# Attention and channel mix in one kernel: new load order, new engine orders, casts moved to GpSimd

## The chip, the cores and the metric

The kernel runs on one core of a Trainium2 chip. Its time is the device time of one launch in microseconds (us). The engines are TensorE (PE; PEld is its weight load), VectorE (DVE), ScalarE (ACT), GpSimd (POOL) and SyncE (SP, which issues the DMAs here). Each engine runs its own instructions strictly in the order in which the program lists them, and waits on semaphores for what other engines and DMAs produce.

## The reference

Windowed attention with a few sink positions is followed by a gated channel mix with a token shift. There are 4 batches, 8 heads, 768 positions, head size 64; the window is 128, and the first 4 positions are seen by all.

```python
scores = scale * np.matmul(q, k.transpose(0, 1, 3, 2))
keep = is_sink | in_window
a = softmax(np.where(keep, scores, -1e9))
x = np.matmul(a, v)                     # to (B, S, H * D)
x_prev = shift(x)                       # one position back, zero first
xk = mu_k * x + (1.0 - mu_k) * x_prev
xr = mu_r * x + (1.0 - mu_r) * x_prev
k = np.maximum(xk @ w_k, 0.0)
v = k * k @ w_v
out = 1.0 / (1.0 + np.exp(-(xr @ w_r))) * v
```

Inputs and output are float32; the kernel computes in bfloat16 with float32 accumulation.

## The kernel before, in words

The work is cut into 12 units of 256 positions, three to each batch. A unit goes through these steps, with the lines of the kernel before:

- load: q, k and v of the unit come by DMA from SP's queue, two DMAs of 256 KB each (v at L304; k and q at L334, or at L314 where a DMA transposes them later: k from unit 4 on, q from unit 8 on). The weights w_k, w_r, w_v come in five DMAs of 1 MB (L351).
- prepare: casts to bfloat16 of k and q (L540, L533: tiles kb and qb) and of v (L643: vb). k and q are transposed on PE with a copy out of PSUM (L573, L586: kt and qt), or by DMA (L559).
- attend: scores on PE into a pair of PSUM tiles (L718), the exponential on ACT (L772, tile e), the mask on DVE (L786), values on PE (L805) with a column of ones that gives the sum, its reciprocal and the product on DVE (L819, L822, tile x). The sink positions add scores (L693, L700) and values (L760), and come from a spread of v (L673, L677).
- mix: x is transposed on PE (L846) and copied to xt (L855), or by DMA for the last three units (L866). DVE makes the difference td of neighbours (L874) and xk and xr from it (L885).
- ffn: the keys product (L936), a relu (L946 on ACT, L950 on DVE), its square (L964 on ACT, L960 on DVE, tile kk), the gate product (L976) with a tanh (L982), the values product (L994; L906 for the very last half), the gating on DVE (L1003; L916) and the store (L1010; L921).

The weights are cast to bfloat16 at L498 (ACT), L502 and L504 (DVE, POOL).

All these steps are recorded as numbered operations (Plan.op) in the order of the program text, and issued in another order, which the table ORDER lists by number; a planner wrote it down ahead of time, and nothing of the planner is left in the kernel. CHOICE names the engine for operations that have several (alts), by number. SLOTS gives the buffer of each taken tile. Since every engine and queue works in order, only the order within each engine matters in ORDER. A negative number in ORDER stands for a matmul of zeros into one of four PSUM banks (Plan.fill, L1014), which computes nothing that is used. PSUM holds two pairs of banks for scores (pool sc) and four single banks (pool bank).

Operations 0 to 3 are the loads of k and q of unit 0; 4 and 5 are v of unit 0; 6 to 9 are k and q of unit 1; 10 and 11 are the two loads of w_k.

Of the kernel before, what the change touches and what calls it, by code (L numbers as in the profile page):

```python
# [18 lines left out]
    90: "ACT", 91: "ACT", 92: "ACT", 93: "ACT", 95: "ACT", 97: "ACT", 99: "ACT", 100: "DVE",  # L19
    103: "DVE", 108: "DVE", 109: "POOL", 111: "DVE", 112: "ACT", 113: "ACT", 139: "DVE", 142:  # L20
    "DVE", 144: "DVE", 145: "DVE", 148: "DVE", 151: "DVE", 154: "DVE", 196: "POOL", 199: "POOL",
    202: "POOL", 206: "DVE", 223: "DVE", 227: "DVE", 228: "ACT", 278: "DVE", 283: "DVE", 284:
    "POOL", 287: "ACT", 288: "DVE", 300: "DVE", 309: "ACT", 313: "ACT", 320: "DVE", 356: "DVE",
    358: "POOL", 363: "POOL", 366: "ACT", 367: "ACT", 369: "DVE", 389: "ACT", 446: "DVE", 447:
    "ACT", 527: "DVE", 548: "ACT", 552: "ACT", 555: "DVE", 560: "ACT", 595: "DVE", 597: "DVE",
    600: "POOL", 602: "DVE", 605: "ACT", 606: "DVE", 628: "ACT", 636: "ACT", 677: "POOL", 681:
    "DVE", 683: "DVE", 684: "DVE", 702: "ACT", 706: "ACT", 710: "ACT", 714: "ACT", 753: "DVE",
    759: "DVE", 761: "ACT", 782: "DVE", 783: "ACT", 787: "ACT", 791: "ACT", 795: "ACT", 832:
    "DVE", 838: "ACT", 839: "ACT", 859: "ACT", 866: "DVE", 867: "ACT", 906: "POOL", 912: "DVE",
    914: "ACT", 915: "DVE", 931: "ACT", 935: "ACT", 939: "ACT", 943: "ACT", 1000: "DVE", 1004:  # L30
    "DVE", 1005: "ACT", 1008: "DVE", 1009: "ACT", 1028: "DVE", 1037: "ACT",
# [116 lines left out]
class Plan:  # L148
# [23 lines left out]
    def run(self):  # L172
        keys = [(name, key) for o in self.ops for name, key in o["take"]]
        for (name, key), slot in zip(keys, SLOTS, strict=True):
            self.buf[key] = self.pools[name][slot]
# [8 lines left out]
def kernel(  # L184
# [14 lines left out]
    nc = tc.nc  # L199
# [14 lines left out]
    P = Plan()  # L214
# [854 lines left out]
```

## Time and profile before

| what | value |
|---|---|
| three runs | 167.81, 171.39, 171.4 us, median 171.39 |
| the profiled execution, from its first instruction to its last | 167.6 us (the profile gives no other time of it) |
| granted TensorE clock | 0.999 |
| DMA packets | 79042, 34.60 MB |

The table of busy times and the views of the profile stand in the prediction. In the views by stage each engine has its busy time and, in brackets, its count of instructions. In the list of groups a row holds line, engine, operation, tiles, shape and count, then busy time and mean duration in ns, then idle time just before the group's instructions and what ended it. In the chain of waits and in the timeline the first two numbers are start and duration in us; x2 means that two instructions that follow each other are merged. In a row of one tile, three durations with slashes are least, median and most, in ns.

### The profile page before, as it was taken

What the parts mean: (1) busy time and instruction counts of PE and PEld (TensorE: products, weight loads), DVE (VectorE), ACT (ScalarE), POOL (GpSimd) and SP (SyncE); (2) the same over time, 40 slices, a digit from 0 to 9 for tenths busy, and PEclk for the clock granted to TensorE, in tenths of its full rate; (3) what the DMA queues carried; (4) which work ended last, traced back from release to release, by engine and by line L of the source; (5) the groups of instructions that cost most, each with busy time, mean ns of one, the idle gap of its engine ahead of it and who ended that gap; (6) DMA issues with size and microseconds to landing.
All of it is one profiled execution on the core that took longest, in us unless ns stands there. A gap on an engine that the chain in (4) does not pass through costs nothing.

```text
span 167.6 us, 4210 instructions
## 1 busy us (share of the span) xinstructions
PE 159.7 (95%) x1601; PEld 102.4 (61%) x1601; DVE 146.2 (87%) x375; ACT 133.4 (80%) x221; POOL 16.6 (10%) x43
## 2 busy tenths in 40 slices
PE   6999997999999999899999999999999999999991
PEld 1447574755558576676556885665765576764850
DVE  5189999999999999899999999989798799998821
ACT  4269998999999997999879999989799829614340
POOL 6423021005000010022000000010010000000000
PEclk9999999999999999999999999999999999999999
DMA  4999989999899999979999999999997774131303
GB/s 102 300 327 369 346 172 312 372 324 328 189 248 166 204 294 224 253 153 133 218 256 149 214 239 174 233 219 200 211 189 185 194 162 155 63 66 63 125 0 125
DMA packets 79042, 34.60 MB, mean 206 GB/s; under 512 B 67112, under 2 KB 73520, under 8 KB 79024
## 3 DMA queue, kind: packets, MB, share of 16 engines
q1 hardware_dynamic: 79008, 34.35, 92.0%
q8 instruction: 12, 0.20, 0.5%
q14 instruction: 6, 0.05, 0.1%
q10 hardware_dynamic: 16, 0.00, 0.0%
HBM read 24.12 MB, written 6.29 MB: 181 GB/s over the span
## 4 chain that ended last, share of the span: by engine, by line
PE 58%; DVE 11%; DMA 11%; SPq 7%; ACT 7%; issue 3%; ACTq 0%; DVEq 0%
PE bank L936 18%; PE bank L994 18%; PE bank L976 8%; DMA vs<-in_v_dram 6%; SPq L334 5%; PE sc L718 4%; PE bank L805 4%; DMA qs<-in_q_dram 3%; ACT e L772 3%; DMA qt<-qb 2%; DVE ob L1003 2%; DVE e L786 2%; PE bank L846 2%; DVE x L822 2%; PE bank L573 2%
## 5 line engine op out<-in xcount | busy, mean ns | idle before, releaser
L936 PE MATMUL bank<-xk,wk_sb 128*128 128x256 bf16 x384 | 48.1, 273 | 0.1
L994 PE MATMUL bank<-wv_h,kk 128*128 128x512 bf16 x184 | 46.4, 379 | 0.0
L772 ACT ACTIVATE e<-sc 128x1024 bf16<-128x1024 f32 (+1 forms) x48 | 45.4, 974 | 1.2 <-PE sc L718 1.2
L936 PEld LDWEIGHTS <-wk_sb 128*128 128x128 bf16 x384 | 36.2, 98 | 7.6 <-issue 0.7
L786 DVE TENSOR_TENSOR e<-e,mask 128x1024 bf16<-128x1024 bf16 (+1 forms) x48 | 30.7, 655 | 0.7 <-ACT e L772 0.5
L946 ACT ACTIVATE rl<-bank 128x512 bf16<-128x512 f32 x38 | 22.4, 616 | 8.6 <-PE bank L936 8.5
L994 PEld LDWEIGHTS <-kk 128*128 128x128 bf16 x184 | 16.6, 98 | 14.4 <-issue 0.3
L976 PE MATMUL bank<-wr_sb,xr 128*128 128x512 bf16 x96 | 23.8, 379 | 0.0
L885 DVE SCALAR_TENSOR_TENSOR xr<-td,mu_all,xt 128x256 bf16<-128x256 bf16 x48 | 22.5, 482 | 0.0
L885 DVE SCALAR_TENSOR_TENSOR xk<-td,mu_all,xt 128x256 bf16<-128x256 bf16 x48 | 21.3, 477 | 0.1
L964 ACT ACTIVATE kk<-rl 128x512 bf16<-128x512 bf16 x26 | 16.7, 649 | 5.3 <-DVE rl L950 5.3
L822 DVE TENSOR_TENSOR x<-bank,rec 128x256 bf16<-128x256 f32 x48 | 19.2, 416 | 0.3
L1003 DVE SCALAR_TENSOR_TENSOR ob<-th,bank 128x512 f32<-128x512 f32 x23 | 15.7, 681 | 4.2 <-PE bank L994 3.3
L805 PEld LDWEIGHTS <-e 128*128 128x128 bf16 x352 | 14.4, 97 | 5.8 <-DVE e L786 1.0
L805 PE MATMUL bank<-vb,e 128*128 128x65 bf16 x352 | 16.9, 193 | 0.8 <-DVE e L786 0.8
L982 ACT ACTIVATE th<-bank 128x512 f32<-128x512 f32 x24 | 14.3, 616 | 3.6 <-PE bank L976 3.5
L1014 PE MATMUL bank<-warm 128*128 128x512 bf16 x44 | 13.8, 440 | 1.5 <-DVE warm L1032 1.1
L718 PE MATMUL sc<-qt,kt 64*128 64x128 bf16 (+1 forms) x256 | 13.9, 237 | 0.3 <-DMA qt<-qb 0.2
L976 PEld LDWEIGHTS <-xr 128*128 128x128 bf16 x96 | 8.9, 98 | 8.6
L718 PEld LDWEIGHTS <-kt 64*128 64x128 bf16 x256 | 9.3, 94 | 4.5 <-issue 3.0
L874 DVE TENSOR_TENSOR td<-xt 128x512 bf16<-128x512 bf16 x24 | 10.1, 425 | 0.8 <-ACT xt L855 0.8
L855 ACT COPY xt<-bank 128x512 bf16<-128x512 bf16 x15 | 9.1, 608 | 1.8 <-PE bank L846 1.8
(72 smaller groups left out, 157.9 us busy)
## 6 DMA issues: line engine op xcount, KB each, us to landing
vs<-in_v_dram SPq DMA_DIRECT2D x24, 256.0 KB, 5.0
ks<-in_k_dram SPq DMA_DIRECT2D x24, 256.0 KB, 5.6
qs<-in_q_dram SPq DMA_DIRECT2D x24, 256.0 KB, 5.1
out_dram<-ob SPq DMA_DIRECT2D x23, 256.0 KB, 2.9
w<-in_moe_w_k_dram SPq DMA_DIRECT2D x2, 1024.0 KB, 7.3
w<-in_moe_w_v_dram SPq DMA_DIRECT2D x2, 1024.0 KB, 8.6
w<-in_moe_w_r_dram SPq DMA_DIRECT2D x1, 1024.0 KB, 7.1
kt<-kb SPq DMA_TRANSPOSE x16, 4.1
```

Source lines behind the costliest of these rows:

```text
L718: nc.tensor.matmul(out=sc[:, a, o0:o1], lhsT=lhs[rows], rhs=rhs[rows], start=u not in BIAS, stop=True, skip_group_check=u in BIAS)
L772: nc.scalar.activation(out=buf[ek][:, :, lo:], in_=buf[sck][:, :, lo:], func=AF.Exp, scale=scale)
L786: nc.vector.tensor_tensor(out=at, in0=at, in1=m, op=ALU.mult)
L805: nc.tensor.matmul(out=o[:, g, a, :], lhsT=e[:, a, e0:e0 + 128], rhs=rhs, start=(T == 0 and i == 0), stop=(i == len(blocks) - 1), skip_gro ...
L822: P.op("DVE", dve(256), lambda ok=ok, rk=rk, c=c: nc.vector.tensor_tensor(out=buf["x", u][:, :, 128 * c:128 * c + 128].rearrange("p g (a d ...
L885: nc.vector.scalar_tensor_tensor(out=buf[key][:, c, :], in0=buf[tk][:, i, :], scalar=mu[w][:, c:c + 1], in1=xt[:, c, t0 - 1:t0 + 255], op0 ...
L936: nc.tensor.matmul(out=ps[:, i, :], lhsT=wk_sb[:, c, 128 * f:128 * f + 128], rhs=xk[:, c, :], start=(c == 0), stop=(c == NC - 1), skip_gro ...
L946: nc.scalar.activation(out=buf[rk], in_=buf[psk].rearrange("p (i t) -> p i t", i=2), func=AF.Relu)
L964: nc.scalar.activation(out=buf["kk", u][:, 2 * f2:2 * f2 + 2, :], in_=buf[rk], func=AF.Square)
L976: nc.tensor.matmul(out=buf[psk], lhsT=buf["xr", u][:, c, 128 * g:128 * g + 128], rhs=wr_sb[:, c, :], start=(c == 0), stop=(c == NC - 1))
L994: nc.tensor.matmul(out=buf[psk], rhs=wv_h[:, f, :], lhsT=buf["kk", u][:, f, 128 * g:128 * g + 128], start=(f == 0), stop=(f == NF - 1))
L1003: P.op("DVE", dve(512), lambda psk=psk, tk=tk, bk=bk: nc.vector.scalar_tensor_tensor(out=buf[bk], in0=buf[tk], scalar=1.0, in1=buf[psk], o ...
```

## The change

Three tables are replaced as a whole (CHOICE, ORDER, SLOTS), and the zero matmul gets a second size. No operation is added or taken away but the zero matmuls.

- SP's queue: q and k of units 0 and 1 come first (eight DMAs), then v of unit 0, q and k of unit 2, v of unit 1, then w_k (two), w_r, and then unit 3, with w_v after its q and k and the v of unit 2. Before, half of v of unit 0 came first, and w_k's two DMAs stood after 12 and 14 DMAs of 256 KB; now 16 stand before the first. Later on the order differs in places.
- Engines, as counts before and after: casts of q and k on ACT 22 and 7, DVE 16 and 3, POOL 10 and 38; casts of v on ACT 11 and 2, DVE 9 and 2, POOL 4 and 20; casts of w_k and w_r on ACT 5 and 0, DVE 1 and 0, POOL 0 and 6; copies to xt on ACT 15 and 10, DVE 3 and 8; relus on ACT 38 and 42, DVE 10 and 6; squares on ACT 26 and 32, DVE 22 and 16.
- PE: all scores of units 0, 1 and 2 stand ahead of the first keys product; before, those of units 0 and 1. The zero matmuls were 44 of 512 columns; now they are 6 of 512 and 69 of 128. All are ahead of the first keys product in both.

```diff
 CHOICE = {
-    90: "ACT", 91: "ACT", 92: "ACT", 93: "ACT", 95: "ACT", 97: "ACT", 99: "ACT", 100: "DVE",
...
+    90: "POOL", 91: "POOL", 92: "POOL", 93: "POOL", 94: "POOL", 95: "POOL", 97: "ACT", 99:
...
 ORDER = (
-    4, 80, 77, 0, 81, 79, 78, 82, 1, 2, 85, 3, 112, 84, 8, -1, -2, -3, -4, -1, -2, 88, 83, 6,
...
+    78, 77, 79, 81, 2, 3, 103, 0, 1, 80, 82, 83, 84, 109, -1, -2, -3, -4, -1, -2, -7, -8, -5,
+    -6, -7, -8, -5, -6, -7, -8, 104, 105, 100, 88, -7, -8, -7, -8, -7, 101, 106, -8, -8, -8,
...
+        banks = self.pools["bank"]
         for i in ORDER:
             if i < 0:
-                self.fill(self.pools["bank"][-1 - i])
+                self.fill(banks[(-1 - i) % len(banks)], 512 if -i <= len(banks) else 128)
             else:
                 self.ops[i]["emit"]()
...
-    P.fill = lambda bank: nc.tensor.matmul(out=bank, lhsT=warm[:, 0:128], start=True,
-                                           rhs=warm.unsqueeze(1).to_broadcast([128, 2, 256]),
-                                           stop=True)
+    def zeros(bank, n):
+        nc.tensor.matmul(out=bank[:, 0:n], lhsT=warm[:, 0:128], start=True, stop=True,
+                         rhs=warm.unsqueeze(1).to_broadcast([128, 2, 256]) if n == 512 else
+                         warm[:, 0:n])
+
+    P.fill = zeros
```

Lines behind the tables stand 2 to 7 further down in the changed kernel: L504 becomes L508, L540 L544, L643 L647, L786 L790, L885 L889, L936 L940, L994 L998, and the zero matmul L1019.

More of the change, by code (lines that the diff above doesn't have):

```diff
@@ L18 @@
 CHOICE = {
-    90: "ACT", 91: "ACT", 92: "ACT", 93: "ACT", 95: "ACT", 97: "ACT", 99: "ACT", 100: "DVE",
[L20 to L30, printed above, removed]
@@ L31 @@
-    "DVE", 1005: "ACT", 1008: "DVE", 1009: "ACT", 1028: "DVE", 1037: "ACT",
+    90: "POOL", 91: "POOL", 92: "POOL", 93: "POOL", 94: "POOL", 95: "POOL", 97: "ACT", 99:
+    "ACT", 105: "DVE", 106: "POOL", 108: "DVE", 109: "POOL", 112: "DVE", 113: "DVE", 139:
+    "POOL", 141: "DVE", 142: "POOL", 145: "POOL", 147: "DVE", 148: "POOL", 154: "DVE", 193:
+    "POOL", 196: "POOL", 199: "POOL", 202: "POOL", 228: "ACT", 236: "ACT", 275: "POOL", 278:
+    "DVE", 281: "POOL", 284: "POOL", 293: "DVE", 309: "ACT", 317: "ACT", 321: "ACT", 358:
@@ new lines @@
+    "POOL", 361: "POOL", 363: "POOL", 369: "DVE", 385: "ACT", 397: "ACT", 436: "POOL", 441:
+    "POOL", 443: "POOL", 449: "DVE", 469: "ACT", 473: "ACT", 516: "DVE", 518: "POOL", 521:
+    "POOL", 523: "POOL", 548: "ACT", 552: "ACT", 556: "ACT", 560: "ACT", 595: "POOL", 597:
+    "POOL", 600: "POOL", 602: "POOL", 615: "DVE", 624: "ACT", 628: "ACT", 632: "ACT", 636:
+    "ACT", 675: "POOL", 677: "POOL", 681: "POOL", 683: "ACT", 686: "DVE", 693: "DVE", 701:
+    "DVE", 702: "ACT", 706: "ACT", 710: "ACT", 753: "POOL", 755: "DVE", 757: "POOL", 759:
@@ L32 @@
+    "POOL", 762: "ACT", 767: "DVE", 786: "DVE", 791: "ACT", 795: "ACT", 830: "POOL", 832:
+    "POOL", 834: "POOL", 858: "DVE", 859: "ACT", 863: "ACT", 867: "ACT", 906: "POOL", 908:
+    "POOL", 912: "POOL", 931: "ACT", 935: "ACT", 943: "ACT", 996: "DVE", 1000: "DVE", 1001:
+    "ACT", 1005: "ACT", 1009: "ACT", 1025: "ACT", 1036: "DVE",
 }
```

160 rows, old and new, of tables (ORDER, SLOTS) are left out of this document.

## The prediction

> **What bounds the kernel now.** I read the page's first part, then the engines' busy time by stages, the chain of waits, and the first 32 us of the timeline.
>
> ```profile
> span 167.6 us, 4210 instructions
> PE 159.7 (95%) x1601; PEld 102.4 (61%) x1601; DVE 146.2 (87%) x375; ACT 133.4 (80%) x221; POOL 16.6 (10%) x43
> ```
>
> ```profile
> core 0: us, PE busy (x) PEld busy (x) DVE busy (x) ACT busy (x) POOL busy (x), PEclk, DMA share, GB/s
> 0.00:30.00 30.00, 27.00 (x260) 15.53 (x262) 23.30 (x68) 21.96 (x34) 9.45 (x29) 1.00 0.95 278
> 30.00:60.00 30.00, 30.00 (x317) 19.44 (x312) 29.57 (x75) 29.69 (x52) 2.85 (x5) 1.00 1.13 257
> 60.00:100.00 40.00, 39.18 (x458) 27.23 (x457) 38.18 (x103) 36.70 (x63) 2.74 (x5) 1.00 1.14 211
> 100.00:131.00 31.00, 30.70 (x306) 19.14 (x306) 27.43 (x69) 28.91 (x49) 1.57 (x4) 1.00 1.10 202
> ```
>
> From 30 to 131 us PE is busy 99.9 of 101 us. DVE (95.2 of 101) and the DMA engines (share above 1) are nearly full too; POOL is empty. So there is nothing to win in the middle, unless PE gets there earlier. How much work PE holds follows from the pace of its long runs in the chain:
>
> ```profile
> 30.58 3.65 PE bank L936 x32
> 34.23 1.73 PE bank L976 x8
> 35.96 0.55 PE sc L718 x12
> 37.59 0.48 PE bank L805 x16
> 42.78 0.45 PE bank L573 x8
> 127.46 3.35 DMA qt<-qb
> 130.86 0.62 PE sc L718 x12
> 163.89 0.42 DVE ob L916
> ```
>
> One matmul of L936 takes 0.11 us, of L976 and L994 0.216, of L718 0.046, of L805 0.03, of L573 and L846 0.056. Times the counts of the program (384, 96 and 184, 256, 352, 96 and 72, and 5 us of small ones) that is about 143 us without the zero matmuls; both kernels have it. The last 3.7 us (163.89 to the end) are the last product's way out. What is left, about 20 us, is time in which PE does nothing useful, and most of it lies at the start:
>
> ```profile
> 1.13 2.74 PE L1014 MATMUL bank<-warm 128*128 128x512 bf16 x6 [1.13 <-DVE warm L1032]
> 10.58 0.50 PE L718 MATMUL sc<-qt,kt 64*128 64x256 bf16 x8
> 21.41 2.78 PE L936 MATMUL bank<-xk,wk_sb 128*128 128x256 bf16 x24
> 30.42 1.85 PE L936 MATMUL bank<-xk,wk_sb 128*128 128x256 bf16 x14
> ```
>
> First scores at 10.58, first keys product at 21.41, and the keys of unit 1 at 30.42. Before that last point PE has done only 12.5 us of work (counts of its list times the pace above): 18 us are lost by 30 us, and 2 to 3 us later.
>
> **The change, part by part.**
>
> *Loads.* q and k of unit 0 are now the first four DMAs, where one of v stood first. First scores need these, a cast, a transpose and a copy (0.6 us each), so they should come about 3 us sooner, near 7.5 us. The w_k loads now have 16 issues of 256 KB ahead of them, not 12 (first half): 1.05 MB more, about 3 us at the 371 GB/s of 15 to 20 us (row below). The first cast of w_k starts at 17.9 before the change (row below too), so I estimate a landing near 20 us. w_r stands ahead of the third unit's v, and comes earlier; w_v about 1 us later, with PE work at hand.
>
> *PE's order.* Scores of units 0, 1 and 2 all stand ahead of the first keys product: 64 matmuls of L718, 56 of L805, 48 of L573 and 28 small ones, 9.3 us of work, where 5.8 us stood there. Keys of unit 1 stand behind 13.0 us (12.5). On the way of this order lie ACT's exponentials and copies:
>
> ```profile
> 11.12 1.51 ACT L772 ACTIVATE e<-sc 128x768 bf16<-128x768 f32 x2 [0.90 <-PE sc L718]
> 16.08 1.98 ACT L772 ACTIVATE e<-sc 128x1024 bf16<-128x1024 f32 x2
> 17.90 1.11 ACT L498 ACTIVATE wk_sb<-w 128x1024 bf16<-128x1024 f32 x1
> 15.00:20.00 5.00, 4.92 (x68) 3.24 (x66) 4.81 (x16) 5.00 (x8) 0.83 (x2) 1.00 1.06 371
> 20.00:25.00 5.00, 4.71 (x50) 3.30 (x47) 4.87 (x10) 5.00 (x9) 1.10 (x2) 1.00 0.94 186
> ```
>
> Between the first scores and the scores that stand right ahead of the keys, ACT has 4 exponentials of 768 columns (0.75 each), 6 of 1024 (0.95), 7 copies and a few small ones (0.5): about 13 us, and some 1.5 us of waits for q of unit 1 and v of unit 0. So keys of unit 0 can start at 7.5 + 14.5 = 22 us, and those of unit 1, 3.7 us of PE work later, at 26. That point lies at 31 us in the kernel before (30.42 and 0.5 us more work). One end: 4.9 us won. ACT may do this since the weight casts left it.
>
> *Choices of engine.* 38 of the 48 casts of q and k (10 before), 20 of the 24 of v (4) and six weight casts go to POOL; POOL gains 44 casts of 512 and six of 1024 columns.
>
> ```profile
> L946 ACT ACTIVATE rl<-bank 128x512 bf16<-128x512 f32 x38 | 22.4, 616 | 8.6 <-PE bank L936 8.5
> L643 ACT CAST vb<-vs 128x512 bf16<-128x512 f32 x11 | 7.0, 648 | 1.0 <-DMA vs<-in_v_dram 1.0
> L533 ACT CAST kb<-ks 128x512 bf16<-128x512 f32 x11 | 6.9, 629 | 1.3 <-DMA ks<-in_k_dram 1.2
> L498 ACT ACTIVATE wk_sb<-w 128x1024 bf16<-128x1024 f32 x4 | 4.6, 1142 | 0.0
> L643 DVE CAST vb<-vs 128x512 bf16<-128x512 f32 x9 | 3.8, 421 | 0.0
> L950 DVE TENSOR_SCALAR rl<-bank 128x512 bf16<-128x512 f32 x10 | 6.8, 683 | 0.5 <-PE bank L936 0.3
> L960 DVE TENSOR_TENSOR kk<-rl 128x512 bf16<-128x512 bf16 x22 | 9.2, 435 | 0.5 <-ACT rl L946 0.5
> L540 POOL CAST qb<-qs 128x512 bf16<-128x512 f32 x6 | 4.9, 833 | 19.9 <-DMA qs<-in_q_dram 19.9
> ```
>
> ACT loses 24 casts (0.64) and five weight casts (1.1), 21 us; it takes 4 relus and 6 squares from DVE and gives it 5 copies of xt, at 0.62 each 3 us more, 18 us less in all. DVE loses 20 casts (0.42), a weight cast (0.69), 4 relus (0.68) and 6 squares (0.43) and takes 5 copies (0.42): 12.3 us less. POOL gets about 44 x 0.62 + 6 x 1.24 = 35 us and has room. But a POOL cast is not free for DVE:
>
> ```profile
> 23.90 0.62 POOL L643 CAST vb<-vs 128x512 bf16<-128x512 f32 x1 [8.07 <-DMA vs<-in_v_dram]
> 25.02 0.81 POOL L643 CAST vb<-vs 128x512 bf16<-128x512 f32 x1
> 25.27 1.09 DVE L786 TENSOR_TENSOR e<-e,mask 128x1024 bf16<-128x1024 bf16 x1
> 39.04 1.70 DVE L786 TENSOR_TENSOR e<-e,mask 128x1024 bf16<-128x1024 bf16 x2
> L786 DVE TENSOR_TENSOR e<-e,mask 128x1024 bf16<-128x1024 bf16 x32 | 22.1, 708 | 0.2
> L885 DVE SCALAR_TENSOR_TENSOR xr<-td,mu_all,xt x48: 452/476/815, 18.8 to 156.8; 128x256 bf16<-128x256 bf16 x48
> L874 DVE TENSOR_TENSOR td<-xt x24: 394/419/622, 17.3 to 151.9; 128x512 bf16<-128x512 bf16 x24
> ```
>
> A mask that began 0.25 us into a cast of 0.81 us took 1.09, not 0.68: DVE lost 0.41, and the cast was itself held up (0.81 for 0.62). The longest xr and td, and the second mask after 39.04, stand beside POOL casts too. These four cost DVE 0.41 + 0.34 + 0.2 + 0.42 (1.70 for two of 0.64) = 1.4 us, over POOL's 14 casts of 512 columns 0.1 us each; 0.42 is the most that one cost. The Trainium skill, page "SBUF — State Buffer", section on the two separate sides, says that the pair of ports shared by the two engines is a lock, held for the whole instruction, with the loser fully blocked. The trace agrees that one waits, but 0.41 us is less than the 0.56 us that the cast still had to run.
>
> In the start this works against the end found above. Six casts of 1024 columns run on POOL from about 20 us on, just while DVE (97% busy there) makes xk and xr; at twice 0.41 us each DVE falls 4.9 us behind, the keys of unit 1 wait, and nothing is won. Ends: 4.9 and 0 us won. I take the middle, 2.5: unit 0's work is mostly done before those casts, and products read from PSUM lie between the steps.
>
> In the middle, counting a weight cast as two, 56 casts at 0.10 to 0.41 us give DVE 5.6 to 23 us back, against 12.3 less: 6.7 less to 10.7 more. DVE has 5.8 us idle between 30 and 131, so PE loses 0 to 4.9 us, and cannot gain over 1.1 (its own idle time there). At 0.25 each DVE's sum changes by 2 us, inside its idle time; I take 1.0 us for collisions that hit a step PE waits for.
>
> *Zero matmuls.* 44 of 512 columns become 6 of 512 and 69 of 128: 44 x 0.216 = 9.5 us become about 2.7 (the first six, by their row) and 69 x 0.056 = 3.9 us. They stand in waits for q, k, v and exponentials; I cost them at nothing. Without that cover they would cost 3.9 us at most, and the old ones 9.5, so no loss against before. If PE ran at the slow pace of its first six (0.46 each) in the waits, the 9.3 us of early work would still fit ahead of 22 us.
>
> *The last unit's loads.* All q, k and v of 12 units go through one SP queue. Unit 11's scores waited for the DMA of qt (chain, 127.46 to 130.86), and stand behind the same PE work in both. The new order has one v load less ahead (near 1.2 us), and SP may wait less for casts:
>
> ```profile
> SPq L559 <- ACT qt L586: 3.4, 2, 2.4
> ```
>
> SP's transposes wait for casts that stood behind such ACT work; POOL makes them as data lands, but in its own order, so that a late v load holds the k cast behind it. If qt still lands at 130.86, no gain remains; with the load less and prompter casts I allow up to 3.0 us.
>
> **Sum.** 167.6 - 2.5 + 1.0 = 166.1 us of span. The page gives no time of its own for the profiled execution; the lowest run, 167.81, is 0.2 above its span, and the median, 171.39, 3.8. Carried to the median: 171.4 - 1.5 = 169.9 us.
>
> **The rivals.**
> *Full start, faster.* POOL's casts miss DVE's steps, the start gives its 4.9, the last unit lets 3.0 through, or more if SP's waits go. For it: the idle ACT and POOL time; against it: DVE at 97% and the DMA share. 171.4 - 3.0 = 168.4, or 164.8 if the time lies by the lowest run as the span does. It is faster by over 2% from 3.4 us.
> *The lock, slower.* Each POOL cast costs DVE its 0.41: 23 - 12.3 - 5.8 = 4.9 us in the middle, and nothing won at the start: 176.3. For it: the 0.41 and DVE at 99% from 30 to 60; against it: the average of 0.1. It decides from (12.3 + 5.8) / 56 = 0.32 us a cast, and reaches 2% at 0.38. A hold of the whole cast, 0.62, would give 34.7 - 18.1 = 16.6 us more, 188. That is the skill's rule at its strongest; I give it little.
> *The loads, no change.* qt of unit 11 lands as now, and what the start wins is waited for there: 171.4.
>
> **How the numbers follow.** Two per cent, 3.4 us, is about what a measurement of this kernel can tell from no change (its three runs differ by 2.1%). Forecast, 0.4: 168.0 to 172.4. Loads bind, 0.12. Full start, 0.28, faster. Lock, 0.2, slower. Same is 0.4 + 0.12 = 0.52. The range, 164.8 to 174.4, takes in the first, the full start and the lock up to 3 us.
>
> **What would show it.** Right: scores near 7.5 us, keys of unit 1 between 26 and 31, weight casts on POOL beside long xk steps, PE full after 31, DVE's busy time near 146. Wrong: masks and xk long all through 30 to 131 with PE idle (lock); a PE wait for qt of over 2 us near 128 (loads); keys of unit 1 by 26 and nothing given back (full start).

## The result, and the profile after

| | before | after |
|---|---|---|
| runs on the same chip, us | 167.81, 170.65, 171.39, 171.4 | 173.75, 174.23, 174.37, 174.96 |
| median | 171.02 | 174.3 |
| the profiled execution's span | 167.6 | 171.2 |
| granted TensorE clock in it | 0.999 | 0.980 |

The changed kernel takes 1.0311 times as long (95% interval 1.021 to 1.0412). It is slower by 3.3 us between the medians (1.9%), where 1.5 us faster was forecast. The ratio goes by fast runs alone, and three of the four runs before lie some 3 us above the first, which is why it is larger than that of the medians; the experiments below are compared by such ratios, to runs of the kernel before on their own chip.

The busy times, and the same four stages as in the prediction:

```profile
span 171.2 us, 4304 instructions
PE 159.0 (93%) x1632; PEld 105.2 (61%) x1632; DVE 149.0 (87%) x349; ACT 120.7 (71%) x197; POOL 58.6 (34%) x93
```

```profile
core 0: us, PE busy (x) PEld busy (x) DVE busy (x) ACT busy (x) POOL busy (x), PEclk, DMA share, GB/s
0.00:30.00 30.00, 23.87 (x290) 17.28 (x291) 22.64 (x58) 18.50 (x28) 19.09 (x39) 0.89 0.91 271
30.00:60.00 30.00, 28.10 (x284) 18.86 (x282) 28.28 (x61) 24.41 (x44) 12.03 (x17) 1.00 0.86 221
60.00:100.00 40.00, 39.43 (x429) 25.94 (x427) 38.43 (x94) 33.76 (x55) 16.73 (x22) 1.00 1.08 224
100.00:131.00 31.00, 30.53 (x314) 20.03 (x313) 28.81 (x68) 24.78 (x42) 9.46 (x13) 1.00 1.19 212
```

PE, which was busy all of 30 to 60 us, now idles 1.9 us there, and its clock was halved for part of the first 30 us (mean 0.89). Behind 60 us the two kernels look alike. ACT was relieved (133.4 to 120.7 us, where 18 us less was meant), but DVE, which was to lose 12.3 us of work, is busy 2.8 us longer.

Busy time mixes zero matmuls with work, so I use another measure, called *PE's loss* below: the start of an instruction minus the PE work that stands ahead of it, at the prediction's paces and without zero matmuls. (Some traces lack up to a tenth of the 512-column matmul records; there their work is scaled to the full count.)

| PE's loss, us | by 21 | by 25 | by 30 | by 40 | by 150 |
|---|---|---|---|---|---|
| before | 15.6 | 15.9 | 17.9 | 18.1 | 20.6 |
| after | 14.7 | 17.7 | 19.1 | 21.5 | 24.8 |

At 21 us the changed kernel is 0.9 us ahead. It then loses 4.3 us on the other between 21 and 40 us, and 0.8 us later on. The places, on PE's timeline:

```profile
9.60 0.82 PE L722 MATMUL sc<-qt,kt 64*128 64x256 bf16 x8
25.31 0.59 PE L1019 MATMUL bank<-warm 128*128 128x128 bf16 x5 [1.69 <-DVE x L826]
28.00 1.45 PE L940 MATMUL bank<-xk,wk_sb 128*128 128x256 bf16 x8
33.51 1.69 PE L940 MATMUL bank<-xk,wk_sb 128*128 128x256 bf16 x14 [1.11 <-DVE xk L889]
```

First scores come at 9.60 us (10.58 before, 7.5 forecast), but the keys of unit 0 at 28.0 (21.41 before, 22 forecast at the early end) and those of unit 1, the 33rd matmul of L940, at 32.13 (30.42 before, 26 to 31 forecast). Both long waits end on DVE. DVE and POOL at that time, and the chain of waits:

```profile
21.67 0.48 DVE L889 SCALAR_TENSOR_TENSOR xk<-td,mu_all,xt 128x256 bf16<-128x256 bf16 x1
23.83 1.09 DVE L889 SCALAR_TENSOR_TENSOR xk<-td,mu_all,xt 128x256 bf16<-128x256 bf16 x1
25.51 1.76 DVE L889 SCALAR_TENSOR_TENSOR xk<-td,mu_all,xt 128x256 bf16<-128x256 bf16 x2
```

```profile
23.04 5.13 POOL L508 CAST wk_sb<-w 128x1024 bf16<-128x1024 f32 x4 [1.57 <-DMA w<-in_moe_w_k_dram]
30.12 2.22 POOL L508 CAST wr_sb<-w 128x1024 bf16<-128x1024 f32 x2 [1.95 <-DMA w<-in_moe_w_r_dram]
```

```profile
19.98 1.01 DVE e L790
21.00 0.75 DVE td L878
22.55 1.20 DVE e L790 x2
23.91 1.01 DVE xk L889
28.07 1.38 PE bank L940 x8
30.33 1.12 DVE td L878
32.54 0.92 DVE xk L889
36.77 1.54 DVE xr L889 x3
38.65 0.61 DVE e L790
```

An xk of 0.48 us takes 1.09 beside a weight cast, and the chain runs on DVE nearly without a break. Against their undisturbed lengths, DVE's steps are 12.7 us longer in all (1.8 before), 7.4 us of it between 10 and 40 us. POOL's first weight cast waits for w_k until 23.04 us.

### The profile page after: what moved, and what is told of

Read it like the earlier page. It is cut to its first block, busy times and chain, and to the rows that moved or that the text cites. A ratio compares the mean times of both kernels' runs of the same rounds, so it can differ in the third digit from the quotient of the medians.

```text
span 171.2 us, 4304 instructions
## 1 busy us (share of the span) xinstructions
PE 159.0 (93%) x1632; PEld 105.2 (61%) x1632; DVE 149.0 (87%) x349; ACT 120.7 (71%) x197; POOL 58.6 (34%) x93
## 4 chain that ended last, share of the span: by engine, by line
PE 67%; DVE 22%; issue 3%; DMA 3%; ACT 2%; SPq 1%; DVEq 0%; ACTq 0%
PE bank L998 21%; PE bank L940 18%; PE bank L980 10%; DVE e L790 6%; PE bank L809 5%; PE sc L722 5%; DVE xr L889 5%; DVE xk L889 3%; DMA ks<-in_k_dram 3%; DVE td L878 2%; PE bank L577 2%; PE bank L850 2%; SPq L338 1%; DVE x L826 1%; DVE ob L1007 1%
## 5 line engine op out<-in xcount | busy, mean ns | idle before, releaser
L940 PE MATMUL bank<-xk,wk_sb 128*128 128x256 bf16 x384 | 48.7, 274 | 1.7 <-DVE xk L889 1.1
L776 ACT ACTIVATE e<-sc 128x1024 bf16<-128x1024 f32 (+1 forms) x48 | 44.6, 965 | 5.4 <-PE sc L722 5.4
L998 PE MATMUL bank<-wv_h,kk 128*128 128x512 bf16 x184 | 44.1, 379 | 0.0
L940 PEld LDWEIGHTS <-wk_sb 128*128 128x128 bf16 x384 | 36.6, 98 | 9.5 <-issue 2.8
L950 ACT ACTIVATE rl<-bank 128x512 bf16<-128x512 f32 x42 | 24.3, 599 | 21.2 <-PE bank L940 20.9
L790 DVE TENSOR_TENSOR e<-e,mask 128x1024 bf16<-128x1024 bf16 (+1 forms) x48 | 31.7, 683 | 0.6 <-ACT e L776 0.5
L647 POOL CAST vb<-vs 128x512 bf16<-128x512 f32 x20 | 16.1, 807 | 36.9 <-DMA vs<-in_v_dram 22.9
L998 PEld LDWEIGHTS <-kk 128*128 128x128 bf16 x184 | 16.9, 98 | 17.7
L889 DVE SCALAR_TENSOR_TENSOR xk<-td,mu_all,xt 128x256 bf16<-128x256 bf16 x48 | 25.6, 563 | 0.4
L889 DVE SCALAR_TENSOR_TENSOR xr<-td,mu_all,xt 128x256 bf16<-128x256 bf16 x48 | 24.2, 525 | 0.1
L968 ACT ACTIVATE kk<-rl 128x512 bf16<-128x512 bf16 x32 | 19.7, 637 | 0.2
L809 PE MATMUL bank<-vb,e 128*128 128x65 bf16 x352 | 16.8, 195 | 0.9 <-DVE e L790 0.5
L537 POOL CAST kb<-ks 128x512 bf16<-128x512 f32 x12 | 9.4, 787 | 17.1 <-DMA ks<-in_k_dram 10.5
L878 DVE TENSOR_TENSOR td<-xt 128x512 bf16<-128x512 bf16 x24 | 13.2, 558 | 0.7 <-DMA xt<-x 0.2
```

Source lines behind the costliest of these rows:

```text
L776: nc.scalar.activation(out=buf[ek][:, :, lo:], in_=buf[sck][:, :, lo:], func=AF.Exp, scale=scale)
L790: nc.vector.tensor_tensor(out=at, in0=at, in1=m, op=ALU.mult)
L809: nc.tensor.matmul(out=o[:, g, a, :], lhsT=e[:, a, e0:e0 + 128], rhs=rhs, start=(T == 0 and i == 0), stop=(i == len(blocks) - 1), skip_gro ...
L889: nc.vector.scalar_tensor_tensor(out=buf[key][:, c, :], in0=buf[tk][:, i, :], scalar=mu[w][:, c:c + 1], in1=xt[:, c, t0 - 1:t0 + 255], op0 ...
L940: nc.tensor.matmul(out=ps[:, i, :], lhsT=wk_sb[:, c, 128 * f:128 * f + 128], rhs=xk[:, c, :], start=(c == 0), stop=(c == NC - 1), skip_gro ...
L950: nc.scalar.activation(out=buf[rk], in_=buf[psk].rearrange("p (i t) -> p i t", i=2), func=AF.Relu)
```

## The experiments

Three explanations stood at the outset. *Lock*: POOL's weight casts hold DVE back in the start. *Order*: whoever casts, the loads and orders put w_k and unit 0's keys too late. *Clock*: the narrower zero matmuls let PE's clock fall to half twice. Each edit is short; the numbers in CHOICE and ORDER are operation numbers (90 to 95 are the casts of w_k and w_r).

**First set: lock, order and clock one at a time.**

The weight casts of the changed kernel from POOL to ACT:

```diff
 CHOICE
-    90 to 95: "POOL"
+    90 to 95: "ACT"
 ORDER      # at these five places behind exponentials and relus of units 0 to 2
+    258, 91, 90;  250, 92;  270, 93;  265, 94;  231, 95
```

> The changed kernel with the six 1024-wide weight casts of w_k and w_r on ACT instead of POOL, placed behind the exponentials after which ACT stands idle (24.6 to 26.4 us in the trace after); POOL then casts only heads, and the other orders stay. By the lock (POOL's wide casts hold back DVE's steps, 7.4 us of lengthening between 10 and 40 us, most of it beside these six), xk falls back toward 0.48 us beside them, the keys of unit 1 start before 32 us, and the time falls by 2 to 4 us, to 170 to 172 us. By the order (all scores of units 0 to 2 are put ahead of the keys, and w_k lands 6 us later than before), the keys can't start earlier whoever casts, and the time stays within 1 us of 174.3. By the clock (two windows of 3.4 us at 0.5) it also stays near 174, since the waits that ended in those windows are still there.

Measured: 174.18 us, 1.0351 (1.0289 to 1.0412). Nothing is won. But DVE's lengthening between 10 and 40 us did fall, from 7.4 to 3.9 us, and PE's loss by 40 us from 21.5 to 20.6. The chain shows what took its place:

```profile
25.13 0.94 ACT wk_sb L502
27.05 0.94 ACT wk_sb L502
28.67 1.16 ACT wk_sb L502
31.73 0.94 ACT wr_sb L502
33.15 0.94 ACT wr_sb L502
```

So this run moved the cost to another engine, and does not acquit the casts.

More zero matmuls in the changed kernel's waits:

```diff
 ORDER
     ... -7, -8, -7, -8, -7,
+    -8, -7, (twelve times)
     101, 106, ...
     ... -7, -7, -7, -7, -7, -7,
+    -7, (twenty times)
     182, 185, ...
```

> The changed kernel with 44 more zero matmuls of 128 columns: 24 in the wait before the first keys of unit 0 are transposed (6.5 to 8.1 us) and 20 in the wait of 23 to 25 us, into banks that are free there. By the clock (the two windows at 0.5, 8.4 to 11.8 and 25.5 to 28.9 us, delayed what followed), the granted clock stays at 1.0 in both windows and the time falls by 1.5 to 3 us, to 171.3 to 172.8 us. By the lock and by the order, PE was waiting on DVE and on late data in and after those windows, so that a full clock only lengthens its waits: within 0.7 us of 174.3.

Measured: 174.12 us, 1.0359 (1.0291 to 1.0427). The clock rose and the time did not move. The changed kernel first, then this one:

```profile
8.00:12.00 4.00, 3.90 (x41) 3.34 (x42) 1.69 (x4) 2.64 (x5) 2.21 (x5) 0.57 1.14 279
25.00:29.00 4.00, 3.69 (x39) 2.80 (x39) 3.93 (x10) 1.86 (x3) 3.17 (x3) 0.57 1.06 375
```

```profile
8.00:12.00 4.00, 3.46 (x49) 2.59 (x51) 2.25 (x5) 2.93 (x5) 2.65 (x5) 1.00 1.17 286
25.00:29.00 4.00, 2.54 (x41) 2.00 (x40) 3.97 (x9) 1.69 (x3) 3.14 (x4) 1.00 1.16 323
```

At full clock PE is busy 1.15 us less in the second window and waits that much more. The clock theory falls.

The two kinds of POOL casts, each alone, in the kernel before:

```diff
 CHOICE
-    90: "ACT", 91: "ACT", 92: "ACT", 93: "ACT", 95: "ACT",      # 94 by default on DVE
+    90 to 95: "POOL"
```

> The kernel before with only the engine of the six weight casts changed, from ACT (five) and DVE (one) to POOL, at their places in the old order. By the lock, DVE's mask, td, xk and xr steps of 17 to 31 us lengthen by 3 to 4 us in all beside 7.5 us of wide POOL casts, the keys of unit 1 come 2 us or more later than 30.4 us, and the time rises by 2 to 4 us. By the order, ACT is relieved of 5.7 us in the start and PE waits no longer than before: within 1 us of the kernel before, or faster.

Measured: 170.49 us, 1.0091 (1.0046 to 1.0136), some 1.5 us slower; PE's loss by 40 us is 20.5 (18.1). Each of the six casts ends earlier here than in the kernel before (the last of w_k at 26.45 us against 26.93, the last of w_r at 30.87 against 32.92), so late weights are not the reason: the lock is real here, though smaller than the 2 to 4 us expected. Some of the steps it hit, and the casts beside them:

```profile
18.83 1.25 DVE L886 SCALAR_TENSOR_TENSOR xr<-td,mu_all,xt 128x256 bf16<-128x256 bf16 x1
20.74 2.05 DVE L886 SCALAR_TENSOR_TENSOR xk<-td,mu_all,xt 128x256 bf16<-128x256 bf16 x3
29.89 1.26 DVE L875 TENSOR_TENSOR td<-xt 128x512 bf16<-128x512 bf16 x1
```

```profile
17.17 2.63 POOL L505 CAST wk_sb<-w 128x1024 bf16<-128x1024 f32 x2 [1.47 <-DMA w<-in_moe_w_k_dram]
20.88 1.23 POOL L505 CAST wk_sb<-w 128x1024 bf16<-128x1024 f32 x1 [1.07 <-DMA w<-in_moe_w_k_dram]
28.59 2.28 POOL L505 CAST wr_sb<-w 128x1024 bf16<-128x1024 f32 x2 [1.59 <-DMA w<-in_moe_w_r_dram]
```

```diff
 CHOICE      # kernel before: the 22 casts of q, k, v from unit 3 on that the change moves
-    595: "DVE", 597: "DVE", 602: "DVE", 681: "DVE", 753: "DVE", 759: "DVE", 832: "DVE", 912: "DVE",
+    275, 281, ... 595, 597, 602, ... 681, ... 753, 759, ... 832, ... 912: "POOL"
```

> The kernel before with the 22 casts of heads that the change moves to POOL from unit 3 on moved, at their places in the old order; the start and the weight casts stay as before. By the forecast's middle term (each 512-wide cast costs DVE 0.1 to 0.4 us, and 60 us of the middle are full of PE work) the time rises by 0.5 to 1.5 us. By a lock that counts everywhere (12.7 us of lengthening in the whole run, 5.3 of it after 40 us) DVE becomes late in the middle too and the time rises by 3 us or more. If DVE's lengthening falls in its own idle time, no change within 0.5 us.

Measured: 169.25 us, 1.0032 (0.9993 to 1.0071). Not told from zero, and at most 1.2 us: these 22 of the 44 casts of heads that move are cheap, as the forecast's middle term had it.

**Second set: orders against engine choices, start against rest.** A splice takes the first steps of one kernel, then the other's order for all that is left; buffers are kept, bar up to four.

```diff
-ORDER, CHOICE of one kernel
+ORDER = first 300 of before, rest of after        # and: first 324 of after, rest of before
+CHOICE = each step as in the kernel it is taken from
```

> The first 300 steps of the kernel before (its loads, orders, zero matmuls and engine choices to about 36 us), then the changed kernel's orders and choices for all that is left; four buffers of 622 moved. If the loss lies in the start (the trace after has 3.4 us more PE idling by 40 us than the trace before), this falls back to within 1 us of the kernel before, plus at most 1 us for the casts of heads on POOL. If it lies in the rest (POOL's casts beside DVE from 40 us on), it stays 3 to 5 us above the kernel before, near 174.

Measured: 172.55 us, 1.0197 (1.012 to 1.0275).

> The reverse: the first 324 steps of the changed kernel, then the orders and choices of the kernel before for the rest; one buffer of 622 moved. If the loss lies in the start, 2.5 to 4 us above the kernel before; if in the rest, within 1 us of it.

Measured: 173.85 us, 1.0293 (1.0215 to 1.037). Neither is near the kernel before. PE's loss by 40 us follows the start (18.9 and 21.3), but both lose 2.8 and 2.9 us between 40 and 55 us, at the seam, where steps of one order meet the other's. With 12 steps out of place instead of 21 it was worse:

> The kernel before up to the first keys of unit 3 (its first 430 steps, 60 us in its trace), then the changed kernel's orders and choices; 12 steps stand on the other side of the two cuts, where the seam at 36 us had 21. If the change's later part costs 1 us or less (the forecast's middle), this is 0 to 1.2 us above the kernel before, and the 2.7 us that PE lost at 40 to 50 us in the first splice belonged to its seam. If the later part carries a loss of its own, 2 us or more above it.

> The changed kernel up to the first keys of unit 3 (457 steps, 63 us in its trace), then the kernel before. If the loss lies in the start, 3 us or more above the kernel before, near the changed kernel. If it lies behind unit 3, within 1.5 us of the kernel before.

Measured: 173.98 us, 1.0297 (1.0222 to 1.0372), and 176.38 us, 1.0465 (1.0404 to 1.0526). PE loses 5.2 and 4.4 us between 40 and 70 us with its single longest waits, 2.1 and 2.3 us, on DVE. Splices of these orders measure their seams as much as their parts; the four runs tell only that a start of the changed kernel has lost 21.3 to 22.4 us by 40 us and a start of the other 18.0 to 18.9.

```diff
-CHOICE of after
+CHOICE of before      # order and loads of after, weight casts placed as in the run on ACT
```

> The changed kernel's loads and orders with every engine choice of the kernel before (ACT's and DVE's weight casts placed behind the exponentials of unit 2 as in the run with ACT's weight casts). If the orders carry the loss (q, k, scores and attention of unit 1 ahead of the keys of unit 0, w_k after them), it stays at 173 us or more however few casts POOL has, with PE's idling before 35 us as in the trace after. If the engine choices carry it, it falls to 170 to 172 us.

Measured: 242.84 us, 1.4316 (1.4222 to 1.4411), which no theory had. The waits of ACT and SP's queue tell why:

```profile
ACT vb L647 <- DMA vs<-in_v_dram: 13.5, 6, 4.7
ACT kb L537 <- DMA ks<-in_k_dram: 7.2, 3, 4.9
```

```profile
SPq L563 <- DVE kb L537: 21.1, 2, 17.6
SPq L563 <- ACT kb L537: 12.1, 3, 9.9
```

The changed order puts a cast of heads right behind its load, where an idle POOL can wait for the data. On ACT and DVE the same place stops all that stands behind it. An order is made for one set of choices, which also holds the other way:

> The loads and orders of the kernel before with every engine choice of the changed kernel, so 60 casts on POOL. The sum of the two parts measured so far would be 1.5 us for the weight casts and 0.5 us for the heads from unit 3 on, so 2 us above the kernel before with nothing lost by the early casts; if the engine choices carry the loss, 5 us above it (near 174), and if the orders carry it all, within 1 us of it.

Measured: 175.04 us, 1.0344 (1.0295 to 1.0393): 2.2% more than the two kinds of casts cost alone (1.0091 and 1.0032). This pair is no test of which of the two carries the loss.

**Third set: single causes in the start.** w_k late, alone, in the kernel before:

```diff
 ORDER      # SP's queue only; 10 and 11 load w_k, 17 to 20 unit 2's q and k, 12 and 13 unit 1's v
-    19, 5, 20, 10, 17, 11, 18, 12, 13
+    19, 5, 20, 17, 18, 12, 13, 10, 11
```

> The kernel before with one thing changed: the two loads of w_k stand behind q, k of unit 2 and v of unit 1 in the queue, as in the changed kernel, so that they land some 3 to 6 us later (22 to 25 us instead of 17 to 20). If the late weights cost the start, the keys of unit 0 move from 21.4 us to 24 us or later, PE idles 2 us more by 35 us, and the time is 1.5 to 3 us above the kernel before. If what costs is only where the scores, attention and keys stand in the orders, within 0.7 us of it.

Measured: 172.19 us, 1.0206 (1.0148 to 1.0263); keys of unit 0 at 25.78 us, PE's loss by 40 us 21.6. One wait on ACT, and behind it one on PE, carry it:

```profile
ACT wk_sb L498 <- DMA w<-in_moe_w_k_dram: 3.7, 1, 3.7
```

```profile
PE bank L1014 <- ACT xt L855: 3.6, 1, 3.6
```

The load lands 4.8 us later (first half at 21.66 us against 16.85), the cast stands in ACT's line, and the copy to xt behind it.

```diff
 both of the edits above in the kernel before: w_k late, 90 to 95 on POOL
```

> The kernel before with both single edits that cost something: w_k's loads behind q, k of unit 2 and v of unit 1 (alone 3.3 us), and the six weight casts on POOL (alone 1.5 us). If they are two costs that add, 4.5 to 5.5 us above the kernel before, which is all that the change lost. If they are the same wait (DVE's xk and w_k both hold the keys of unit 0), 2.5 to 3.7 us above it, and the last 1 to 2 us of the change's loss lie elsewhere. If w_k's lateness cost only because ACT's queue stood still behind the cast (3.7 us of waiting in the trace), POOL takes that wait and it falls to 1.5 to 2 us.

Measured: 171.25 us, 1.0158 (1.01 to 1.0215). The two do not add (1.030 would be the sum); POOL can wait for w_k without holding anyone's copies. So in the kernel before, the change's weight handling costs 1.0 to 2.2%, not all of the loss.

The early q and k, alone:

```diff
 ORDER      # kernel before; 4 loads the first half of v
-    4, ..., 0, 1, 2, 3, 8, 6, 7, 9
+    0, 1, 2, 3, 8, 6, 7, 9, 4      # its cast 112, the spread 115 and the sinks' step 116 later
```

> The kernel before with the forecast's one sure gain alone: the first load of v behind q and k of units 0 and 1 (its cast on ACT, the spread matmul and the sinks' step on DVE moved behind the first scores). By the forecast, the first scores come 0.65 us or more earlier than 10.6 us and up to that much is kept, so 0.3 to 0.8 us faster. If the start is bound by DVE's and ACT's work ahead of 21 us, not by when q and k land, within 0.3 us of the kernel before.

Measured: 169.08 us, 1.0024 (0.9985 to 1.0063). This kernel read the sinks' sums before they were made, so a wait is missing in it; with that step behind its matmul:

> The kernel before with the first load of v behind q and k of units 0 and 1, with its cast, the spread matmul and, behind that, the sinks' step moved after the first scores (in the run before this one the sinks' step was emitted ahead of the matmul that it reads). By the forecast up to 0.7 us of earlier scores are kept: 0.3 to 0.8 us faster. If the start is bound by DVE's and ACT's work ahead of 21 us, within 0.4 us of the kernel before.

Measured: 169.79 us, 1.0043 (1.0008 to 1.0079); scores at 9.31 us, keys of unit 0 at 22.1. Scores 1.3 us earlier are worth nothing, or less.

The changed kernel repaired by hand (keys of unit 0 and w_k ahead again), and its first 20 us followed by the other's order:

```diff
 ORDER      # on the run with ACT's weight casts
+    5, 10, ... 18, 11 (loads);  156, 157, 164, 163 (the four xk);  251, 221, 222, 225, 226 (keys)
```

> The changed kernel with the weight casts on ACT and, besides, the keys of unit 0 put ahead again: w_k's first load behind v of unit 0, its casts on ACT at 18 us, the four xk of unit 0 on DVE and its 32 key matmuls on PE ahead of unit 1's division by the sums. The early scores stay. If the order of keys and w_k carries the start's loss, the keys of unit 0 start at 21 to 23 us instead of 27, PE's idling by 40 us falls from 20.6 to 18 or 19 us, and the time falls to 171 to 172.5 us. If the loss is the sum of DVE's and ACT's work by then, whichever comes first, it stays at 174.

Measured: 180.14 us, 1.0662 (1.0603 to 1.0721), the wrong way for both theories. With w_k ahead, v of unit 1 is late instead, and PE, whose keys I had left behind unit 1's values, waits for its cast:

```profile
25.01 0.38 PE L809 MATMUL bank<-vb,e 128*128 128x65 bf16 x4 [2.53 <-POOL vb L647]
```

```diff
+ORDER = first 146 of after (loads of w_k, unit 2 and unit 1's v as in before), rest of before
```

> The changed kernel up to the first xk of unit 0 (about 20 us: q and k of units 0 and 1 first, early scores, its engine choices), then the orders and choices of the kernel before, with w_k's loads between q and k of unit 2 and the weight casts on ACT as there. If the loss of the start is w_k and the keys of unit 0 coming late, and the early scores are worth something, PE's idling by 40 us is 17 to 18.5 us and the time is from 1.5 us below to 0.5 us above the kernel before. If the early scores push the other loads back by as much as they win, it is 1 to 3 us above the kernel before.

Measured: 170.02 us, 1.0024 (0.9979 to 1.007), though with runs from 168.03 to 172.49 us. The changed kernel's first 20 us are no better than the other's. In the profiled execution (170.32 us) they cost something: PE's loss by 40 us is 2.6 us above that of the kernel before, against the 17 to 18.5 us expected, and 1.3 us above it by 150 us. Its one long wait is that of the run with w_k late: ACT waits 3.0 us for w_k, whose cast starts at 20.62 us (17.90 before), and PE for the copy to xt behind it:

```profile
22.20 1.01 PE L577 MATMUL bank<-ident,qb 128*128 128x128 bf16 x8 [3.39 <-ACT xt L859]
```

w_k stands behind 12 loads there, as in the kernel before, and yet was issued at 11.36 us (9.55 before).

**Fourth set: no weight casts at all.** The six casts left out, the weights zeroed once, in both kernels:

```diff
+            if name != "wv":
+                return lambda: nc.vector.memset(wk_sb if name == "wk" else wr_sb, 0.0)
 CHOICE
+    90 to 95: "DVE"
 ORDER
-    90 to 95 at their places
+    90, 94 behind 80 and 81
```

> The changed kernel without the six casts of w_k and w_r: the two bfloat16 tiles are zeroed once by DVE at 3 to 6 us and the loads land unread, so the two products work on zeros. This takes away at once POOL's wide casts beside DVE, the waits for w_k, and ACT's share of any of it. If the lock and w_k's lateness carry the start's loss, the keys of unit 0 start by 25 us and the time falls by 3 us or more, to 171 us or below. If the order carries it (three masks, two divisions and unit 1's scores and values ahead of unit 0's xk and keys), PE idles as before, 20 us or more by 40 us, and the time stays at 173 to 174.5 us. If the part behind 40 us keeps 1.7 us whatever the start does, the gap to the kernel before without weight casts is at least 1.7 us.

> The kernel before with the same thing left out, as the other's control: five casts of 1.1 us leave ACT and one of 0.7 us leaves DVE, of which some 5 us lie between 18 and 33 us, and the keys of unit 0 no longer wait for w_k. They were bound by xk (21.2 us on DVE), so they start at 20.5 to 21.5 us as now; keys of unit 1 come 1 to 2 us earlier, and the time falls by 0.5 to 2 us, to 167 to 168.5 us. The difference between the two is what the orders, the heads' casts and the other choices cost with no weight cast in either: 5 us if weights play no part, 2 us or less if they carry most of it.

Measured: 170.47 us, 1.0132 (1.006 to 1.0205), and 168.74 us, 1.002 (0.9986 to 1.0055), both to the same runs of the kernel before. Leaving the casts out wins nothing in the kernel before, and in the changed kernel it takes the ratio from 1.0311 to 1.0132 (two sets of runs), about 3 us (1 to 5 by the two intervals). PE's loss by 40 us is 16.8, where the changed kernel has 21.5, the kernel before 18.1 and its twin here 17.7. The same stretch of PE's timeline as above:

```profile
23.97 0.44 PE L1021 MATMUL bank<-warm 128*128 128x128 bf16 x5 [1.05 <-DVE x L828]
25.59 1.05 PE L942 MATMUL bank<-xk,wk_sb 128*128 128x256 bf16 x8
26.81 4.53 PE L942 MATMUL bank<-xk,wk_sb 128*128 128x256 bf16 x40
```

The keys run from 25.6 us without a wait into those of unit 1 (29.43 us). What is left, 1.9 us between the two, lies behind 40 us: this kernel loses 5.4 us from there to 150 us, its twin 2.1. From 60 to 115 us, first this kernel, then its twin:

```profile
60.00:115.00 55.00, 52.71 (x575) 35.14 (x576) 53.15 (x121) 43.13 (x72) 17.41 (x25) 1.00 1.01 217
```

```profile
60.00:115.00 55.00, 54.46 (x613) 37.00 (x610) 52.89 (x138) 51.61 (x88) 4.17 (x6) 1.00 1.20 212
```

DVE is as full in both, though 17 of its instructions are gone here: against their undisturbed lengths its steps are 5.9 us longer between 60 and 110 us, the twin's 1.1. All of this kernel's PE waits from 40 to 131 us that have a name end on DVE (vsink, xk, x, ob; 2.0 us). So with PE in time, DVE seems to hold the later part; those waits are 2.0 of the 5.4 us, and no run tests it alone.

## Why the prediction was wrong, point by point

- *The start, forecast at 2.5 us won, lost 3.4 (PE's loss by 40 us, 21.5 against 18.1).* This is the step that failed. Its ends were 4.9 and 0: I let POOL's weight casts eat the win but not go beyond it, with nothing that excluded a loss. Three prices in it were off. First scores came at 9.6 us, not 7.5, since PE waited for the cast of k at 7.43. The keys of unit 0 were reckoned from ACT's work (22 us); but unit 0's four xk stand on DVE behind masks of unit 1, and a sum of DVE's work in that order was never made; its last xk ends at 27.3 us (21.2 before). One step of them alone, the second in the row at 25.51 us, took 1.25 us instead of 0.48 beside a weight cast. And w_k, put near 20 us, was cast from 23.04 on.
- *The mechanism of the win was right in kind.* With no weight casts in either, PE's loss by 40 us is 16.8 us in this order, 0.9 less than its twin's. The 4.9 us end was not near: even there the keys start at 25.6 us, behind the last xk.
- *The weights cost about 3 us (1.0311 to 1.0132).* That lock and late landing each can cost is shown in the kernel before (1.0091 and 1.0206, together 1.0158). How the 3 us divide between them in the changed kernel stays open: moving the casts to ACT removed half of DVE's lengthening there and put ACT's casts on the chain. DVE's lengthening per POOL cast, 12.7 / 64 = 0.20 us (0.18 with a weight cast counted as two, as the forecast does), was not far below my 0.25, but it is no even price: in the start it fell where wide casts met steps that PE waited for, up to 0.77 us each.
- *The lock's rule was weighed wrongly.* I held 0.41 us lost, with 0.56 us of the cast still to run, against the rule of the Trainium skill (page "SBUF — State Buffer", section on the two separate sides) that the loser waits out the whole instruction. But the mask of my own row ended at 26.36 us, 0.53 after its cast (25.83), with 0.68 us its full length: it had done no more than a start before the cast ended. The rows of the run with weight casts on POOL in the kernel before agree: the xr ends at 20.08, the second xk at 22.39 and the td at 31.15 us, each 0.28 us after a cast's end (19.80, 22.11, 30.87), where the undisturbed step takes 0.42 to 0.48. The trace agrees with the rule; a step that meets a running cast loses what is left of the cast, less 0.15 to 0.2 us. In all 20 traces, every xk, xr and td that a POOL cast lengthened by over 0.1 us, 198 in all, ended 0.27 to 0.28 us after that cast, while DVE's steps that read PSUM beside such casts (x, the reciprocals, the copies to xt) grew by at most 0.01 us.
- *The middle, forecast at 1.0 us lost, lost 0.8* behind 40 us, between the two profiled executions, and 22 of the 44 casts of heads cost at most 1.2 us alone. It was right for a late PE only: with PE in time it is 3.3 us (5.4 against 2.1 in the last two runs). DVE's busy time from 30 to 131 us, forecast between 6.7 us less and 10.7 us more, rose by 0.3 (95.5 against 95.2). My sum set the relief and the casts of the whole kernel against DVE's idle time in this stretch alone; 46 of the 64 POOL casts start in it, and DVE's steps are about 8 us longer there. Which of the later choices this comes from, besides casts, was not separated.
- *Zero matmuls at nothing:* right. They lost the clock twice, and full clock changed nothing.
- *The last unit's loads:* the 3.4 us of the chain were the DMA's own time. PE, which had other work, stood still for qt only 0.23 us before, so no more than that was there to win:

```profile
130.86 0.62 PE L718 MATMUL sc<-qt,kt 64*128 64x256 bf16 x12 [0.23 <-DMA qt<-qb]
```

  No wait for qt is left near the end in the changed kernel, and nothing came through, since PE reached unit 11's scores 4.0 us later than before (134.86 against 130.86 us).
- *The rivals.* The slower one had the right mechanism in the wrong place: it wanted every cast to cost 0.32 us from 30 to 131 us, and in the mean a cast cost 0.18 us by its count; the start was enough. The full start did not come, and the loads did not bind. The measured time, 174.3 us, lies just inside the range, at the bound that the lock had set; that it does is luck, since the bound stood for a loss in the middle.
- *A sum:* the terms of PE's work as I listed them give 139.5 us, not 143 (the 16 matmuls of L906 are not among them). No term of the forecast hangs on it.

## What to carry to other kernels

When an order brings one stage forward, add up, for the step that ends the stage, the work ahead of it on every engine and the landing of every input, and take the latest; I did it for PE and ACT, and not for DVE. A range for a stage with a known adverse effect does not end at zero. And an engine as full as DVE here (95.2 of 101 us before) can turn time won upstream into waits later, so price its lengthened steps with the upstream part already on time.

## What the runs showed of the hardware that I had not expected

PE's clock falls on fixed windows, and a half-busy window is enough. In all traces here the granted clock changes at steps of 3.41 us. In the first 45 us of the 20 traces, every window at full clock in which PE was busy less than 1.8 us (13 of them, 0.44 to 1.79) was followed by one at 0.5; of those with 1.8 us or more one was (2.51 us). Later in the runs, eight windows with up to 1.38 us went the same way, and one with 1.69 us did not. The Trainium skill, page "TensorE: Matmul & The Clock Gate", Part 1, has free-running windows of 3413 ns, with which the traces agree, and a return to half rate after an idle window; here the window was busy for up to half of its length.
